# A new order of the steps of a windowed attention, with merged visits of P times V and four PSUM tiles that are allocated once

## The chip, the cores and the metric

The kernel runs on one core of one Trainium2 chip. The metric is device time in microseconds (us) for one execution. Three runs of the kernel before took 691.85, 692.1 and 692.67 us; their median, 692.1 us, is the time before.

## What is computed

From an input x of 2048 tokens by 512 features the program computes two branches and mixes them by a gate:

```
qkv = x @ wqkv                       # 32 heads of 16 features
scores = q k^T / 4, each token sees itself and the 255 tokens before it
a = softmax(scores) @ v  ->  @ wo
b = gelu(layernorm(x) @ w1 + b1) @ w2 + b2      # 512 -> 1792 -> 512
g = sigmoid(sum(x * gate_w));  out = g * a + (1 - g) * b
```

All of it is in 32-bit floats.

## The kernel before

The program has three stages. The first makes q, k and v and writes q and k to DRAM in stacks. The second is attention, and it is where the change lies. The third multiplies the hidden layer by w2, the attention's result by wo, and writes the output. The third begins when the second's last matmul is through.

The attention stage handles four heads at a time, in eight chunks (`p` from 0 to 7), and 2048 tokens in 16 blocks of 128. It consists of four kinds of step, which TensorE executes in the order of the letters of the string `ORDER` (`run`, L735). The order is thus written out by hand, and it is static: TensorE goes through it in sequence, and a step that waits holds all behind it.

- **S** (`s_pair`, L348) multiplies q of one block with the keys that it sees, 128 to 384 columns, for two heads side by side. VectorE then finds the largest score of each row: a masked copy (L366) and a maximum (L367), or, for the first two blocks of a chunk, two calls of L363 with a read-out each. After each four blocks `put_max` (L371) sends the maxima through POOL, VectorE and DRAM back into the stacks, 6, 13, 21 and 28 steps later (`CHAIN`).
- **T** (`st_pair`, L403) multiplies k with q, transposed, with the maxima already in the product. ScalarE takes the exponential (L414) and POOL masks it (L416).
- **P** (`pv`, L423) multiplies the exponentials with v, for two blocks of queries (a group `j` of eight), 256 columns. Each product is a real 32-bit one, which the trace records as two passes, and four heads go side by side in columns of the array, 32 wide. ScalarE copies the 256 columns to SBUF (VectorE in the last chunk).
- **f** (`fill`, L706) is one of 24 steps of a unit of the hidden layer (`mlp1_unit`, L626; 28 units): two matmuls of 512 columns, which use the two halves of the array's rows. The units hang on nothing in attention, so their steps fill the time in which the others wait.

In all there are 256 T, 236 S (20 more stand in the first stage), 64 P and 672 f. One P is run behind the string, and the last 14 f after it.

The results lie in PSUM in four pairs of banks, `b0` to `b3`. A running unit of f holds one pair; S, T and P take the others in turn, from a list `ring`, whose next entry a digit of the string `PICK` chooses. Each use allocates a new tile on its pair (`ps`, L103), which waits until those who used the pair's former tile are through.

Of the kernel before, what the change touches and what calls it, by code (L numbers as in the profile page):

```python
# [13 lines left out]
F32R = mybir.dt.float32r  # L14
# [23 lines left out]
ORDER = ("TfSfSfffffTfSfffTSfffTfSfffTSfffTfSffSPTSffTfSfffTSfffSPSTfSfffTfSfTffTffTSffTfffTSPSSTPSTfTfffTSffT"
         "ffSffTSffffTSfffTfSffTfSfffSPSTSPTffSTffTfffTfSTffffTSffTfSfffTSfffTfSffSPSSTPTffTSffTffSffTfSfffTSf"
         "ffTfSfffTSfffTfSfSPSTTPTTSPSSTPSffTSffffSTfffTffSffTfSfffTfSffTfSfffSPSTTffffSTffTfffSTffTfffSSPfSfT"  # L40
         "ffSffTfTfffTSPSSTPTffTSfffTfSffTfSffffTSfffTfSffTffSffTPfSSPTffSfTfSffTfSfTffTffSTfffSffTfSfffTSfffS"
         "PTSTPSTSPTffTSffTffSffTSffffTSffffSTfffTffTfSfSfPSSTPfSfTfSfffTfTffSfTfSffffTSfffTfSffffTfSPSTSPTfSf"
         "ffTSfffTfSffTfSfffTfSfTfffTSfTffffTSPTTSPSTSPfTfSTfffSfffTSfffTfSffTfSfffTSfffTfSffSPPSTffTfffSTffTf"
         "ffTfSTfffSfTffTfSffTfSfffSPSSTPSffTfSfffTSfffTfSfffTSfffTfSfffTSffffSPPfSTfTfffSfTffTfSffTffTfSffTff"
         "SfTfTffffSPTTSPSTSPSfffTSfffTfSffTfSffffTSfffTfSffTfSfffSPfSTfTffffTfSTfffTfSfffTSfffTfSffTfSfffSPTS"
         "SPPTSTffffTfSTfffSffTfSfffTSfffTfSffTfffSfSPTSTPSSfTffffTfSffTfSfffTSfffTfSfffTSfffffSTPTTSPTSffTffS"
         "ffTfSfffTSfffTffSfTfTfffSTfTfffSPSSSPPSTSffffTfSfffTSfffTfTfffSTfffTffSTffffSPSTSPSTffTfffSTffTffTSf"
         "ffSffTSfffTfSffTfSfffSPSTSPfTfSTfffTffTSfffTfSfffTSfffTfSffTfSfffSPTTSPSTSPTffTSffTfSfffTfSfffSSfffT"
         "ffffTSffTfSffSPSffTSfffTfSffTfSffSTfffTffTffTfTffffTfPPTTTPfTffTffTffTPPTfTfffTffTfffTTffTfffTfPfTTf"
         "TTffffP")  # L50
PICK = ("0000000000000000001000000000000000000001000100100000000000000000100001000100000000000001000000000000"
        "0000000000000100010000010000000000001001001000101010001000100000000000000000001000000000100000000000"
        "0010000000000001000010020101010000000000100101000000000000000010000001000010000000000000000100100010"
        "1000000000100000000000000000000000000000000000000001000000000000000000010001000000000000001000000100"
        "0000000000000000100000000000000000000000000001001100000010010000000010010000000010000010000000000010"
        "00010000000000000000000101000100000100000000000000010000000000000000000000000000000")
# [5 lines left out]
def gated_mix_kernel(ctx, tc: tile.TileContext, xt, x2, wq0, wqk, wv, wo, xa, gw, w1, w2, b1, b2, out):  # L62
    nc = tc.nc
    dve, act, pool, pe, sp = nc.vector, nc.scalar, nc.gpsimd, nc.tensor, nc.sync
# [38 lines left out]
    def ps(tag, shape=(128, 512)):  # L103
        key, bufs = banks[tag]
        return left[key].tile(list(shape), F32, name=nm("ps_" + tag), tag=tag, bufs=bufs)

    ring, picks = [], list(PICK)

    def choose():
        return ring.pop(int(picks.pop(0)) if picks else 0)  # L110

    def two():
        if not ring:
            return ps("x", (128, 2, 512))
        ring.append(choose())
        return ps(ring[-1], (128, 2, 512))

    def small(tag, bufs, shape, dt=F32):
        return consts.tile(list(shape), dt, name=nm(tag), tag=tag, bufs=bufs)

    def view(t, *ap, off=0):
        return bass.AP(tensor=t.tensor, offset=t.offset + off, ap=[list(x) for x in ap])

    def f32(t):
        return t.bitcast(F32)

# [17 lines left out]
    spot = [None]  # L144
    soons = {}
# [224 lines left out]

    def put_max(p, a):  # L371
        mx = mxs[p][:, :, :, a:a + 4]
        m = small("nm", 2, (128, 2, 2, 2, 4), F32R)
        ms = small("ms", 2, (128, 32))
        md = dram.tile([2, 2, 2, 4, 128], F32R, name=nm("md"))

        def parts():
            pool.tensor_copy(m[:, 0], mx)
            lo_part(m[:, 1], mx, m[:, 0], pool)

        def turn():
            dve.transpose(ms, f32(m).rearrange("p a b c d -> p (a b c d)"))

        def put(eng=None):
            (eng or (act if spot[0] > 99 else sp)).dma_start(f32(view(md, [32, 4], [128, 32], [1, 32])), ms)

        def rest():
            done.add(("m", p, a // 4))
            for k in range(2):
                src = view(md, [512, 2], [1024, 2], [1, 512], off=2048 * k)  # L390
                sp.dma_start(f32(qk[62 + k:113 + k:50, :2, a * 128:a * 128 + 512]), f32(src))

        if spot[0] is None:
# [26 lines left out]
        while late:  # L420
            late.pop(0)()

    def pv(p, j, last):  # L423
        flush()
        a = two()[:, 0]
        parts = ((-1, 0, 128, 256), (-2, 0, 256, 128), (0, 0, 0, 256), (1, 128, 0, 128))[0 if j else 2:]
        for n, (d, at, fr, w) in enumerate(parts):
            kb = 2 * j + d
            for h in range(4):
                v = (4 * p + h) * VW  # L430
                pe.matmul(a[32 * h:32 * h + 32, at:at + w], vs[:, kb, v:v + 32], pts[p, kb][:, h, fr:fr + w],  # L431
                          start=n == 0, stop=n == len(parts) - 1, skip_group_check=True, tile_position=(0, 32 * h))
        if j % 2 == 0:
            sums.append(sums.pop(0))
            acc[p] = sums[-1]
        s = acc[p]
        o = j % 2 * 256
        if last:
            dve.tensor_copy(s[:, o:o + 256], a[:, :256])
        else:  # L440
            copy(s[:, o:o + 256], a[:, :256])
        if j % 2:
            to = osc[p, :, (j - 1) * 256:(j + 1) * 256]
            if lt:
# [180 lines left out]

    def mlp1_unit(f, cp):  # L626
        held = choose()
        o = ps(held, (128, 2, 512))
        w = w1t[f]
        n = 0  # L630
        for k, i in ((0, 0), (1, 0), (0, 1)):
            for kt in range(KT):
                y = ys[cp, i, kt // 4]
                a = kt % 4 * C
                m = kt % 4 * 128
                for e in range(2):
# [95 lines left out]
    ls = [(p, qb, pr) for p in range(8) for qb in range(NB) for pr in range(2)][2 * (NB - LAG):]  # L732
    lp = [(p, j) for p in range(8) for j in range(NB // 2)]

    def run(order):  # L735
        for a in order:
            spot[0] += 1
            for fn in soons.pop(spot[0], []):
                fn()
            flush()  # L740
            if a == "T":
                p, kb, pr = lt.pop(0)
                if not pr:
# [137 lines left out]
    for n in range(len(seq)):  # L881
        tick()
        for k in (n + 6,):
            c, f = item(k)
# [4 lines left out]
        c, f = item(n + 1)  # L889
# [6 lines left out]
        c, f = seq[n]  # L896
# [52 lines left out]
```

## Time and profile before

| | before |
|---|---|
| median of three runs | 692.1 us |
| span of the profiled execution | 687.8 us |
| first stage, to the first step of attention | 144.3 us |
| attention | 343.5 us |
| third stage | 200.0 us |
| TensorE busy | 680.8 us, 99% |
| VectorE, ScalarE, POOL busy | 69%, 56%, 39% |
| granted clock of TensorE | 9 tenths or more in each of 40 slices |

The profile comes from one execution, with a span of 687.8 us; the median of the runs shown stands 4.3 us above it, and those 4.3 us lie outside of what the profile covers. Since matmuls overlap and their ends are modelled, TensorE's busy time hides short waits. They are seen better in the starts of its instructions: a step that begins later than the step before it needs has waited.

### The profile page before, as it was taken

Reading aid. Unit: us, or ns where it says so; the run is one execution under the profiler, and the core shown is the slowest. Engines: PE = TensorE matmul, PEld = TensorE weight load, DVE = VectorE, ACT = ScalarE, POOL = GpSimd, SP = SyncE. Lnnn points to the kernel's source line nnn. Section 1 sums busy time; section 2 is a strip of 40 time slices with the busy share of each in tenths; the row PEclk is TensorE's granted clock in tenths of the full one; section 3 lists DMA queues with packets and bytes.
Section 4 is the critical chain, followed back from the end, with each engine's and each line's share of the span. In section 5 each row is a group of like instructions: output and inputs, shape, how many; then the busy total and the mean of one; then the engine's idle time right before and its main releaser. Section 6 shows DMA issues by size and latency. Waiting matters only on the chain.

```text
span 687.8 us, 15782 instructions
## 1 busy us (share of the span) xinstructions
PE 680.8 (99%) x5738; PEld 536.9 (78%) x5738; DVE 474.4 (69%) x972; ACT 384.9 (56%) x639; POOL 267.1 (39%) x622
## 2 busy tenths in 40 slices
PE   9999999999999999999999999999999999999997
PEld 6887777877877777778787877777788888888886
DVE  6737779967877878778587777866575545556454
ACT  6437453457677686876867767678633224123131
POOL 5800156426566665755666655658000000000000
PEclk9999999999999999999999999999999999999999
DMA  8999887796665758656776555526786450831801
GB/s 313 363 311 267 252 268 248 225 276 203 208 195 171 228 179 261 195 155 229 219 229 190 173 184 167 190 96 218 272 261 199 140 172 5 270 132 44 250 1 62
DMA packets 89621, 137.92 MB, mean 201 GB/s; under 512 B 13160, under 2 KB 36648, under 8 KB 89416
## 3 DMA queue, kind: packets, MB, share of 16 engines
q1 hardware_dynamic: 81384, 128.72, 58.5%
q10 hardware_dynamic: 8160, 8.19, 4.0%
q8 instruction: 46, 0.75, 0.5%
q14 instruction: 31, 0.25, 0.1%
HBM read 81.53 MB, written 54.30 MB: 197 GB/s over the span
## 4 chain that ended last, share of the span: by engine, by line
PE 95%; ACT 2%; DMA 1%; DVE 1%; POOL 1%; issue 0%; SPq 0%; DVEq 0%; ACTq 0%
PE ps_a L858 22%; PE ps_b L638 22%; PE ps_d L303 12%; PE ps_b L431 12%; PE ps_d L333 7%; PE ps_b L412 6%; PE ps_o L827 6%; PE ps_b L357 6%; PE ps_d L290 1%; PE ps_x L357 1%; DMA wv<-in_wq 1%; ACT pb L414 0%; DMA md<-ms 0%; DVE us L872 0%; ACT x L414 0%; ACT t L131 0%
## 5 line engine op out<-in xcount | busy, mean ns | idle before, releaser
L638 PE MATMUL ps_b<-x,w 64*128 64x512 f32 x1344 | 210.8, 395 | 0.2 <-ACT pb L414 0.2
L858 PE MATMUL ps_a<-x,t 128*128 128x512 f32 x648 | 149.7, 389 | 0.0
L367 DVE TENSOR_REDUCE mx<-ps_b 128x2 f32<-128x512 f32 x208 | 144.0, 692 | 7.2
L858 PEld LDWEIGHTS ps_a<-x,t 128*128 128x128 f32 x648 | 121.6, 188 | 25.3
L638 PEld LDWEIGHTS ps_b<-x,w 64*128 64x128 f32 x1344 | 129.0, 186 | 11.2 <-issue 2.0
L366 DVE COPY_PREDICATED ps_b<-tri,ps_b 128x256 f32<-128x256 uint8 x208 | 88.2, 424 | 43.7 <-PE ps_b L357 32.6
L416 POOL TENSOR_SCALAR_AFFINE_SELECT pa<-pa 128x256 f32<-128x256 f32 x192 | 74.3, 415 | 66.7 <-ACT pa L414 66.2
L414 ACT ACTIVATE pa<-ps_b 128x768 f32<-128x768 f32 x96 | 76.6, 813 | 25.6 <-PE ps_b L412 18.9
L412 PE MATMUL ps_b<-qk 64*128 64x384 f32 (+5 forms) x512 | 88.6, 338 | 0.8 <-DMA qk<-md 0.3
L303 PE MATMUL ps_d<-x,w 128*128 128x512 f32 x360 | 84.7, 390 | 0.0
L357 PE MATMUL ps_b<-qk 62*128 62x384 f32 (+2 forms) x472 | 82.5, 343 | 0.2
L303 PEld LDWEIGHTS ps_d<-x,w 128*128 128x128 f32 x360 | 67.3, 188 | 14.5 <-issue 0.5
L416 POOL TENSOR_SCALAR_AFFINE_SELECT pb<-pb 128x256 f32<-128x256 f32 x160 | 62.7, 420 | 39.1 <-ACT pb L414 37.1
L414 ACT ACTIVATE pb<-ps_b 128x768 f32<-128x768 f32 (+2 forms) x96 | 65.5, 706 | 17.2 <-PE ps_b L412 12.0
L694 ACT ACTIVATE t<-t,b1s 128x512 f32<-128x512 f32 x56 | 38.5, 716 | 45.3 <-DMA t<-hp 44.8
L412 PEld LDWEIGHTS ps_b<-qk 50*128 50x128 f32 (+1 forms) x512 | 50.4, 184 | 17.3 <-issue 4.2
L416 POOL TENSOR_SCALAR_AFFINE_SELECT x<-x 128x256 f32<-128x256 f32 x128 | 49.9, 420 | 26.4 <-ACT x L414 26.0
L414 ACT ACTIVATE x<-ps_b 128x768 f32<-128x768 f32 x64 | 51.1, 813 | 13.4 <-PE ps_b L412 10.1
L357 PEld LDWEIGHTS ps_b<-qk 62*128 62x128 f32 (+1 forms) x472 | 45.2, 184 | 16.1 <-issue 3.6
L333 PE MATMUL ps_d<-wv,x 128*128 128x512 f32 x192 | 46.7, 394 | 0.0
L827 PE MATMUL ps_o<-w,t 128*128 128x512 f32 x192 | 46.1, 389 | 0.0
L431 PE MATMUL ps_b<-pa,v 128*32 128x256 f32 (+1 forms) x768 | 43.3, 330 | 0.2 <-POOL x L416 0.2
(96 smaller groups left out, 755.9 us busy)
## 6 DMA issues: line engine op xcount, KB each, us to landing
qk<-qk SPq DMA_DIRECT2D x112, 196.0 KB
t<-hp SPq DMA_DIRECT2D x56, 256.0 KB
hp<-t SPq DMA_DIRECT2D x54, 256.0 KB
qk<-t SPq DMA_DIRECT2D x48, 256.0 KB
osc<-x SPq DMA_DIRECT2D x31, 256.0 KB
t<-in_w SPq DMA_DIRECT2D x28, 256.0 KB
w<-w SPq DMA_DIRECT2D x28, 256.0 KB
qk<-t ACTq DMA_DIRECT2D x24, 256.0 KB
```

The costliest lines, as they stand in the source:

```text
L303: pe.matmul(o, a[:, dt * 128:(dt + 1) * 128], b[:, dt * C:(dt + 1) * C], start=n == 0, stop=n == 11)
L333: pe.matmul(o, x[:, a:a + 128], wvs[dt][:, k], start=n == 0, stop=n == 11)
L357: pe.matmul(o[:, e, :n], qs[pr][r:k, qb * 128:qb * 128 + 128], ks[pr][r:k, t0:t0 + n], start=True, stop=True)
L366: dve.copy_predicated(o[:, :, :128], tri, o[:, :, 256:384])
L367: dve.tensor_reduce(m, o[:, :, :256], mybir.AxisListType.X, ALU.max)
L412: pe.matmul(o[:, e, :w], ks[pr][r:k, kb * 128:kb * 128 + 128], qs[pr][r:k, kb * 128:kb * 128 + w], start=True, stop=True)
L414: act.activation(pt[:, :, :w], o[:, :, :w], AF.Exp, scale=0.25)
L416: pool.affine_select(out=pt[:, :, a:a + 128], in_=pt[:, :, a:a + 128], pattern=[[0, 2], [sgn, 128]], base=b, channel_multiplier=-sgn, comp ...
L431: pe.matmul(a[32 * h:32 * h + 32, at:at + w], vs[:, kb, v:v + 32], pts[p, kb][:, h, fr:fr + w], start=n == 0, stop=n == len(parts) - 1, sk ...
L638: pe.matmul(o[:, e], w[kt // 4][r:r + 64, k, m:m + 128], y[r:r + 64, a:a + C], start=n == 0, stop=n == 23)
L827: pe.matmul(a, x[:, g], wos[g][:, k], start=n == 0, stop=n == 11)
L858: pe.matmul(accs[c][b], x[:, b * 128:(b + 1) * 128], w, start=f == 0 and n == 0, stop=f == FT - 1 and n == 2)
```

## The change

The two strings are new ones. `ORDER` has the same letters in the same numbers (652 f, 256 T, 236 S, 63 P) in another sequence, and `PICK` chooses other banks.

When two P follow each other and the first has an even `j`, they are run as one: `pv` gets `both`, computes 512 columns in one bank with six products in place of eight (four in place of six where `j` is 0), and ScalarE copies the 512 columns in one instruction. In the new string this holds at three places, each of them the groups 0 and 1 of a chunk (chunks 4, 6 and 7).

The four pairs of banks are allocated once, at their first use (`pair`), and then written again as the same tile. `put_max` allocates its two small tiles when they are written and not when the step is reached, and `run` calls all functions that are due at a place or before it, since a merged visit counts for two.

```diff
-ORDER = ("TfSfSfffffTfSfffTSfffTfSfffTSfffTfSffSPTSffTfSfffTSfffSPSTfSfffTfSfTffTffTSffTfffTSPSSTPSTfTfffTSffT"
+ORDER = ("TSTffffSffTSffffTSfffTfSffTffSffTfSfffSPffTSffTffSffSPTfSTfffTffSTffSfTffSTffSffTSfPSTSPTffSTfffSffT"
...
-    ring, picks = [], list(PICK)
+    ring, picks, pairs = [], list(PICK), {}
+
+    def pair(tag):
+        if tag not in pairs:
+            pairs[tag] = ps(tag, (128, 2, 512))
+        return pairs[tag]
...
         ring.append(choose())
-        return ps(ring[-1], (128, 2, 512))
+        return pair(ring[-1])
...
-        m = small("nm", 2, (128, 2, 2, 2, 4), F32R)
-        ms = small("ms", 2, (128, 32))
+        sm = {}
...
-    def pv(p, j, last):
+    def pv(p, j, last, both):
         flush()
         a = two()[:, 0]
-        parts = ((-1, 0, 128, 256), (-2, 0, 256, 128), (0, 0, 0, 256), (1, 128, 0, 128))[0 if j else 2:]
+        if both:
+            parts = ((-1, 0, 128, 256), (-2, 0, 256, 128), (0, 0, 0, 384), (1, 128, 0, 384), (2, 256, 0, 256),
+                     (3, 384, 0, 128))[0 if j else 2:]
+        else:
+            parts = ((-1, 0, 128, 256), (-2, 0, 256, 128), (0, 0, 0, 256), (1, 128, 0, 128))[0 if j else 2:]
...
-        if last:
+        if both:
+            copy(s, a)
+        elif last:
             dve.tensor_copy(s[:, o:o + 256], a[:, :256])
...
     def mlp1_unit(f, cp):
         held = choose()
-        o = ps(held, (128, 2, 512))
+        o = pair(held)
...
+                p, j = lp.pop(0)
+                skip = b == "P" and j % 2 == 0
+                if skip:
+                    lp.pop(0)
+                pv(p, j, not ls, skip)
+                spot[0] += skip
```

Three places of TensorE's order show what moves. In the rows, L638 and L651 are f, L357 and L362 are S, L412 and L418 are T, L431 and L441 are P (lines before and after the change); the digit behind `ps_b` is the pair of banks, and x4 counts equal instructions. Two equal rows of f stand for one step.

The first place is the start of chunk 4's P, before the change two visits on two pairs of banks (b2 and b0):

```order
L638 MATMUL ps_b1_706_4613<-x8_171_1021,w_572_3687 128x512 x8
L357 MATMUL ps_b3_721_4747<-qk_3_79 128x384 x2
L431 MATMUL ps_b2_725_4755<-pa_255_1523,v_4_80 32x256 x4
L431 MATMUL ps_b2_725_4755<-pa_255_1523,v_4_80 32x128 x4
L431 MATMUL ps_b0_726_4765<-pa_255_1523,v_4_80 32x256 x4
L431 MATMUL ps_b0_726_4765<-pa_255_1523,v_4_80 32x128 x4
L431 MATMUL ps_b0_726_4765<-x8_253_1521,v_4_80 32x256 x4
L431 MATMUL ps_b0_726_4765<-pa_255_1523,v_4_80 32x128 x4
L638 MATMUL ps_b1_727_4783<-x8_193_1143,w_571_3686 128x512 x2
```

With the change the same two groups of chunk 4 are one visit, on b0 alone:

```order
L651 MATMUL ps_b2_262_1541<-x8_171_1021,w_358_3470 128x512 x8
L362 MATMUL ps_b3_263_1547<-qk_3_79 128x384 x2
L362 MATMUL ps_b1_261_1536<-qk_3_79 128x384 x2
L441 MATMUL ps_b0_260_1530<-pa_255_1523,v_4_80 32x384 x8
L441 MATMUL ps_b0_260_1530<-x8_253_1521,v_4_80 32x256 x4
L441 MATMUL ps_b0_260_1530<-pa_255_1523,v_4_80 32x128 x4
L362 MATMUL ps_b2_262_1541<-qk_3_79 128x128 x2
L418 MATMUL ps_b3_263_1547<-qk_3_79 128x384 x2
L651 MATMUL ps_b1_261_1536<-x8_193_1143,w_357_3469 128x512 x6
L362 MATMUL ps_b0_260_1530<-qk_3_79 128x128 x2
```

Six groups of four products became four, of the same 1152 columns, and b0 is used again six steps later.

The second place is the end of the string, the last T of chunk 7, on TensorE before the change:

```order
L412 MATMUL ps_b2_1091_7352<-qk_3_79 128x256 x2
L412 MATMUL ps_b3_1092_7357<-qk_3_79 128x256 x2
L638 MATMUL ps_b1_1061_7140<-x8_212_1256,w_874_5787 128x512 x2
L412 MATMUL ps_b0_1095_7374<-qk_3_79 128x128 x2
L412 MATMUL ps_b2_1096_7379<-qk_3_79 128x128 x2
L638 MATMUL ps_b3_1097_7384<-x8_193_1143,w_931_6234 128x512 x8
L431 MATMUL ps_b1_1098_7393<-pa_255_1523,v_4_80 32x256 x4
```

The same four T with the change:

```order
L418 MATMUL ps_b1_261_1536<-qk_3_79 128x256 x2
L418 MATMUL ps_b0_260_1530<-qk_3_79 128x256 x2
L651 MATMUL ps_b3_263_1547<-x8_193_1143,w_465_5770 128x512 x4
L418 MATMUL ps_b2_262_1541<-qk_3_79 128x128 x2
L651 MATMUL ps_b3_263_1547<-x8_193_1143,w_465_5770 128x512 x4
L418 MATMUL ps_b1_261_1536<-qk_3_79 128x128 x2
L651 MATMUL ps_b3_263_1547<-x8_193_1143,w_465_5770 128x512 x8
```

Before, b2 and b3 are taken again one and two steps behind the T that used them; with the change five steps lie between the two uses of b1, and f runs on b3, which neither T has.

The third place is the first S of chunk 2 with the P next to it, shown with the semaphores that each instruction waits for, on TensorE before the change:

```order
L357 MATMUL ps_b3_400_2514<-qk_3_79 128x128 [waits DMAHW7_49,DMAHW6_49,Activation_49]
L357 MATMUL ps_b3_400_2514<-qk_3_79 128x128
L638 MATMUL ps_b0_382_2381<-x8_212_1256,w_233_1370 128x512 x2
L357 MATMUL ps_b1_408_2531<-qk_3_79 128x128 [waits DVE_49,PE_49]
L357 MATMUL ps_b1_408_2531<-qk_3_79 128x128
L431 MATMUL ps_b2_411_2538<-pa_255_1523,v_4_80 32x256 [waits Activation_49,Pool_49]
```

And with the change:

```order
L362 MATMUL ps_b1_261_1536<-qk_3_79 128x128 [waits DMAHW7_49,DMAHW6_49,Activation_49]
L362 MATMUL ps_b1_261_1536<-qk_3_79 128x128
L651 MATMUL ps_b3_263_1547<-x8_212_1256,w_233_1370 128x512 x4
L362 MATMUL ps_b2_262_1541<-qk_3_79 128x128 [waits DVE_49]
L362 MATMUL ps_b2_262_1541<-qk_3_79 128x128
L362 MATMUL ps_b0_260_1530<-qk_3_79 128x256 [waits Activation_49]
L362 MATMUL ps_b0_260_1530<-qk_3_79 128x256
L441 MATMUL ps_b1_261_1536<-pa_255_1523,v_4_80 32x256 [waits DVE_49,Pool_49]
```

P took b2 from a T before, and takes b1 from an S now, four steps behind that S. The wait for TensorE's own semaphore is gone from the second S: over the whole program 263 of TensorE's instructions wait for two semaphores or more before the change, and 125 with it.

## Rows read from the trace of the kernel before

**Rows 1.** The page: busy us of the engines, and TensorE's granted clock in 40 slices.
```profile
PE 680.8 (99%) x5738; PEld 536.9 (78%) x5738; DVE 474.4 (69%) x972; ACT 384.9 (56%) x639; POOL 267.1 (39%) x622
...
PEclk9999999999999999999999999999999999999999
```
**Rows 2.** The page's chain of waits, by line, shares of the span.
```profile
PE ps_a L858 22%; PE ps_b L638 22%; PE ps_d L303 12%; PE ps_b L431 12%; PE ps_d L333 7%; PE ps_b L412 6%; PE ps_o L827 6%; PE ps_b L357 6%; PE ps_d L290 1%; PE ps_x L357 1%; DMA wv<-in_wq 1%; ACT pb L414 0%; DMA md<-ms 0%; DVE us L872 0%; ACT x L414 0%; ACT t L131 0%
```
**Rows 3.** The three stages: length, busy us by engine, clock, DMA share, GB/s.
```profile
0.00:144.30 144.30, 142.62 (x626) 111.30 (x626) 104.07 (x197) 72.31 (x157) 56.66 (x70) 1.00 0.88 280
144.30:487.80 343.50, 342.01 (x4250) 263.59 (x4249) 260.89 (x588) 249.88 (x384) 210.44 (x552) 1.00 0.62 196
487.80:687.80 200.00, 196.13 (x866) 162.02 (x864) 109.46 (x187) 62.70 (x98) 0.00 (x0) 1.00 0.47 151
```
**Rows 4.** TensorE's timeline around one P: start us, length, instructions.
```profile
423.44 0.86 PE L638 MATMUL ps_b<-x,w 64*128 64x512 f32 x6
424.12 0.36 PE L357 MATMUL ps_b<-qk 62*128 62x384 f32 x2
424.41 0.64 PE L431 MATMUL ps_b<-pa,v 128*32 128x256 f32 x8
424.86 0.40 PE L431 MATMUL ps_b<-x,v 128*32 128x128 f32 x8
425.08 0.61 PE L431 MATMUL ps_b<-pb,v 128*32 128x256 f32 x8
425.51 0.40 PE L431 MATMUL ps_b<-x,v 128*32 128x128 f32 x8
425.84 0.45 PE L357 MATMUL ps_b<-qk 62*128 62x384 f32 x2
426.13 0.34 PE L412 MATMUL ps_b<-qk 64*128 64x384 f32 x2
426.31 0.34 PE L357 MATMUL ps_b<-qk 62*128 62x384 f32 x2
```
**Rows 5.** TensorE's timeline at two P in a row, first and next step.
```profile
401.34 0.64 PE L431 MATMUL ps_b<-pa,v 128*32 128x256 f32 x8
...
404.08 0.44 PE L357 MATMUL ps_b<-qk 62*128 62x384 f32 x2
```
**Rows 6.** TensorE's timeline at the last T.
```profile
477.68 0.24 PE L412 MATMUL ps_b<-qk 64*128 64x128 f32 x2
478.25 0.33 PE L412 MATMUL ps_b<-qk 64*128 64x128 f32 x2 [0.33 <-ACT pb L414]
478.74 1.20 PE L638 MATMUL ps_b<-x,w 64*128 64x512 f32 x8 [0.16 <-ACT pb L414]
```
**Rows 7.** TensorE's timeline at a T of chunk 1.
```profile
213.25 0.66 PE L638 MATMUL ps_b<-x,w 64*128 64x512 f32 x4
214.26 0.45 PE L412 MATMUL ps_b<-qk 64*128 64x384 f32 x2 [0.35 <-DMA qk<-md]
```
**Rows 8.** TensorE's timeline at the first S of chunk 2.
```profile
201.64 0.33 PE L357 MATMUL ps_b<-qk 62*128 62x128 f32 x2
202.18 0.86 PE L431 MATMUL ps_b<-pa,v 128*32 128x256 f32 x16 [0.21 <-POOL x L416]
```
**Rows 9.** ScalarE's copies out of PSUM: busy us, mean ns, idle before.
```profile
L131 ACT ACTIVATE t<-ps_b 128x512 f32<-128x512 f32 x54 | 29.4, 599 | 3.3 <-PE ps_b L638 3.2
L131 ACT ACTIVATE x<-ps_b 128x256 f32<-128x256 f32 x56 | 21.6, 385 | 30.0 <-PE ps_b L431 28.3 <-ACT t L131 1.1 <-ACT pb L414 0.5
```
**Rows 10.** VectorE's work for narrow S, in attention.
```profile
L363 DVE CUSTOM_DVE_ANT_0 scr<-ps_b,wide 128x256 bf16<-128x256 f32 x28 | 10.8, 422 | 10.2 <-PE ps_b L357 10.2
L363 DVE CUSTOM_DVE_ANT_0 scr<-ps_b,wide 128x128 bf16<-128x128 f32 x28 | 7.0, 288 | 4.4 <-PE ps_b L357 4.2
...
L363 DVE DVE_READ_ACCUMULATOR2_ANT mx<- 128x1 f32 x56 | 4.6, 83 | 0.0
```
**Rows 11.** Semaphore waits that stand alone on TensorE's queue before S: ns min/median/max.
```profile
L357 PEldq EVENT_SEMAPHORE  x130: 51/51/849, 48.2 to 456.2; - x130
```

More of the change, by code (lines that the diff above doesn't have):

```diff
@@ L37 @@
 U8 = mybir.dt.uint8
-ORDER = ("TfSfSfffffTfSfffTSfffTfSfffTSfffTfSffSPTSffTfSfffTSfffSPSTfSfffTfSfTffTffTSffTfffTSPSSTPSTfTfffTSffT"
[L39 to L56, printed above, removed]
+ORDER = ("TSTffffSffTSffffTSfffTfSffTffSffTfSfffSPffTSffTffSffSPTfSTfffTffSTffSfTffSTffSffTSfPSTSPTffSTfffSffT"
+         "fSfffTSfffTfSfffTSfffTfSffSPTTSPTSfTfffSfTfTfffSTfTffSfTffSfffTSfffTfSffSPSTSPTSTfffTffSTffSfffTSfff"
+         "fTSfffTfSffTffSffSSPTTSPTTSPSSTPSffTfSfffTfSffTfSffffTSfffTfSffTffTffSPSTSPSffTfSfffSTfffTffTfSfTffS"
+         "ffTffSfTfTfffSTPSTTPPSTfffTffSTffSfffTSffffTSfffTfSffTfSfffSPSTffSfTffSTfffSfTSfffTfSffTfSfffTSffffT"
+         "fSPTSTPSSTPSffTfSfffSTfffTffSffTfSfffTSfffTfSfffSPTSTPSTffTfTffSTfffSffTfSfffTSfffTfSffTfffSfSPPTSff"
+         "TffTffSTfffTffSTfffSffTSffTffSTfffSfSPTSTPSSTPSfffTSffffTSffTffSffTffSffSfTfffTfffTSPSSTPTffSffTfSff"
+         "fSfTffTffTffSTfTffSffTSffffSPTSTPTffSTffTfffTSffTffSffffSTfffSffTffffSSPPSTfffSTffSfTffTfSffTfffSTff"
+         "fTffSTfffTffSPSTTPTSTPTSffTffSffTfSffffTSfffTffSfTffSffTffSfSPSffSfTfffTfSfffSfTfffSffTSffffTfSffSfP"
+         "STSPPTSffTffSffTfSfffTSffffSTffSfffTSffSffTSfPTSTPTSfffTfSffTfSfffTSffffTSffTffSffTSffffSPTSTPSTffTf"
+         "ffSTffTfffTSfffTffSfTffSfffTTfffSSPPTSTPTSffTffSffTfSfffTSffffTSfffTfSffTfffSfSPPSTfffTffSTfffSffTSf"
+         "fTfSfTffSfTfSffTfSfffSPSTSPSffTSffffTfSfffTfSffTfSfffTfSffTffffSTPSSTPTffSTfffTffSTffSffTffTfSffTfSf"
+         "ffSTfffSfPSTTPTSfffTfSffTffSffTSffffTSffffSTffTffffTTPPTfffTfffTTPTTffTfPPTTffTffffTfffTfTffTfffTPPT"
+         "TffTffT")
@@ new lines @@
+PICK = ("0000000000000000000100000000100000000000001010010000000000000000000000100110000000000010100000100000"
+        "0000010000100010001100000000000000100101000010001010100000010000100100000000000000000000000000000100"
+        "0000011000010000000000000100110010000000000010000001001001000000000000011000000000010001000110000010"
+        "0010000000000000100000010000000000000000100100100100000000000000001010001001000100000010010100000000"
+        "0010010000000000000000000000000000000100100000101000010000000000000000000000010010010000000000001010"
+        "00000000000000000110010010100000101001000000000000010000000000000000000000001000")
@@ L372, in put_max @@
         mx = mxs[p][:, :, :, a:a + 4]
-        m = small("nm", 2, (128, 2, 2, 2, 4), F32R)
-        ms = small("ms", 2, (128, 32))
+        sm = {}
         md = dram.tile([2, 2, 2, 4, 128], F32R, name=nm("md"))
         def parts():
+            m = sm["m"] = small("nm", 2, (128, 2, 2, 2, 4), F32R)
             pool.tensor_copy(m[:, 0], mx)
@@ L381, in turn @@
         def turn():
-            dve.transpose(ms, f32(m).rearrange("p a b c d -> p (a b c d)"))
+            sm["s"] = small("ms", 2, (128, 32))
+            dve.transpose(sm["s"], f32(sm["m"]).rearrange("p a b c d -> p (a b c d)"))
         def put(eng=None):
-            (eng or (act if spot[0] > 99 else sp)).dma_start(f32(view(md, [32, 4], [128, 32], [1, 32])), ms)
+            (eng or (act if spot[0] > 99 else sp)).dma_start(f32(view(md, [32, 4], [128, 32], [1, 32])), sm["s"])
         def rest():
@@ L441, in pv @@
             copy(s[:, o:o + 256], a[:, :256])
-        if j % 2:
+        if j % 2 or both:
+            j += both
             to = osc[p, :, (j - 1) * 256:(j + 1) * 256]
@@ L735, in run @@
     def run(order):
-        for a in order:
+        skip = False
+        for a, b in zip(order, order[1:] + " "):
+            if skip:
+                skip = False
+                continue
             spot[0] += 1
-            for fn in soons.pop(spot[0], []):
-                fn()
+            for n in sorted(n for n in soons if n <= spot[0]):
+                for fn in soons.pop(n):
+                    fn()
             flush()
@@ L748, in run @@
             elif a == "P":
-                pv(*lp.pop(0), not ls)
+                p, j = lp.pop(0)
+                skip = b == "P" and j % 2 == 0
+                if skip:
+                    lp.pop(0)
+                pv(p, j, not ls, skip)
+                spot[0] += skip
             else:
```

## The prediction

> **What bounds the kernel now.** I read the page first. TensorE is busy for 680.8 of 687.8 us, no other engine for more than 69%, and its granted clock is at the upper of its two levels, 2.4 GHz, throughout [rows 1]. The chain of waits that ended last is TensorE's nearly from end to end, by the lines of its matmuls [rows 2]. The table by stage puts 343.5 us into attention, between 144.3 us of the first stage and 200.0 us of the third, whose code the change leaves alone [rows 3]. So the time is the sum of TensorE's steps in attention and of the waits between them, and I read the steps off its timeline by their starts.
>
> Three f take 424.12 − 423.44 = 0.68 us, so one takes 0.227. A T of 384 columns takes 426.31 − 426.13 = 0.18. In a P, four products side by side take 425.51 − 425.08 = 0.43 us at 256 columns and 425.08 − 424.86 = 0.22 at 128 [rows 4], so a P costs by columns: 2 × (0.43 + 0.22) = 1.3 us for the full form, 0.65 for group 0.
>
> Around a P something is added. The S ahead of it takes 424.41 − 424.12 = 0.29 us and not 0.18; so does the S behind it, 426.13 − 425.84. And the P itself takes 425.84 − 424.41 = 1.43 [rows 4], while two in a row take 404.08 − 401.34 = 2.74, that is 0.12 less than twice 1.43 [rows 5]. An unbroken run of P therefore costs 0.11 + 0.12 + 0.11 = 0.34 us, once, however many P it holds.
>
> The floor of the stage, from the steps' numbers: 672 f × 0.227 = 152.5; 432 S and T of 384 columns × 0.18 = 77.8; 60 narrower ones, at 0.227 us per 512 columns, 5.1; 56 full P × 1.3 and 8 × 0.65, 78.0; 58 runs of P × 0.34 = 19.7. That is 333.1 of 343.5 us. About 10 us are waits and small delays, and that is all that an order can win beyond the runs of P.
>
> **The change, part by part.** *Runs of P.* Counted in the strings, with the P behind them, the P stand in 58 unbroken runs before and in 55 now. Three runs less save 3 × 0.34 = 1.0 us, all on TensorE's path.
>
> *Merged visits.* They save 24 products, 48 recorded passes. In the rows the time of a P is proportional to its columns, 0.43 against 0.22 us for twice the columns [rows 4], and 1152 columns are streamed in either form. I take 0; the bounds are 0 and 3 × 0.3 us saved, if the two narrow groups that go at each place had cost 0.15 us beyond their columns. The Trainium skill (TensorEngine Tiling (Array Packing), Instruction Overhead) gives each matmul about 60 cycles of overhead, so that one of few columns takes as long as one of 60; at 2.4 GHz and 48 passes an estimate from that page is 1.2 us, and the sum would be 688.6. The proportional rows speak against it.
>
> The copy of a merged visit takes 599 ns in place of two of 385 [rows 9]: ScalarE gains 0.17 us three times, off the path. The bank comes free 0.21 us later. At chunk 4 the next user of b0 comes six steps on, behind S, T and three f, over 0.9 us, which covers 0.6. I take 0; without that cover it costs 3 × 0.21 = 0.6 us. The same page (PSUM Bottleneck) warns that column tiling speeds up TensorE but not the emptying of PSUM, which speaks against one wide copy; by it the sum would be 690.3, and the order shows the cover.
>
> *Waits that go.* At the last T of chunk 7, TensorE needs 0.57 and 0.49 us for two steps of 128 columns, a quarter of an f or 0.06 each, because their banks were still with the exponential [rows 6]: 0.94 us. In the new order the pair is used again after five steps, and f has another pair. This wait goes, and nothing stands close behind it: six f, 1.4 us, separate the last T from the last P, which needs its exponential and its mask first.
>
> At 214.26 a T waits for the maxima: 1.01 us for two f, 0.55 too much [rows 7]. By the two strings the T stood 42 steps behind the S that releases the maxima, and stands 45 behind it now; from the step that sends them to DRAM (21 behind the S) to the T I count 5.85 us of steps before and 6.43 now. The 0.58 gained covers 0.55. No other T has less than 6.0 now, and before one with 6.07 came without a wait.
>
> *Waits that stay or come.* At the first S of chunk 2 P waited: 0.54 us for an S of 0.06 plus 0.11, so 0.37 [rows 8]. Now P takes the bank of an S that VectorE needs 2 × 288 + 2 × 83 = 742 ns for [rows 10], 0.64 us behind it. I leave 0.37. Elsewhere old tight places go and new ones come. Counting places where a pair is taken again with less than 0.25 us to spare beyond its reader's duration, I find 19 before and 24 now. I take 0, with ±2 us as bounds.
>
> *Tiles allocated once.* 263 instructions of TensorE waited for two or more semaphores, 125 do now. An extra wait stands alone on the queue for 51 ns [rows 11]. But the S at 424.12 has one (its semaphores are VectorE's and TensorE's), and the f ahead of it still took 0.227; the S at 426.31 has two, and the T ahead took 0.18 [rows 4]. They lie beside running matmuls. I take 0, and keep 154 × 0.051 = 7.9 us as the far bound (154 such waits fewer in the built program). ScalarE gets 88 more; it is busy for 250 of 343.5 us [rows 3], so I take 0 there too.
>
> *The sum,* against the profiled execution: 687.8 − 1.0 − 0.94 − 0.55 = 685.3 us, and with the 4.3 us by which the median stands above that span, 689.6 us, 0.4% less.
>
> **The rivals.** *Queue relief.* If the lone waits do delay weight loads behind them, part of the 7.9 us and of the 10 us of small delays goes as well: half of the 7.9 gives 685.7. For it speaks that some f begin late without a named wait; against it the steps of rows 4, at full pace behind one or two such waits. 14%.
>
> *Nothing left.* The new tight places cost what the old ones did and 2 us more: 691.6, no change that can be told. For it: 24 against 19; ScalarE's queue carries more waits, and a late exponential holds a bank. 25%.
>
> *Banks from narrow S (slower).* Adding up the steps above between the end of an S and the next use of its pair, I find 13 places in the new order with less than 1.16 us, down to 0.64; in the old one 1.16 is the least. The narrow S allow for it, which need 742 ns of VectorE, or 2 × 422 + 2 × 83 = 1010 [rows 10]. But whatever stands in VectorE's queue ahead comes on top. If each place then holds TensorE for 0.6 us, 7.8 us come and the time is 697.4. It decides from 0.3 us a place: 13 × 0.3 = 3.9 us is the gain of 2.5 and the 1.4 that cannot be told. For it: VectorE is busy for 261 of 343.5 us [rows 3]. Against it: beyond the 742 or 1010 ns, ten of the 13 places leave 0.12 us or more, and from one S to the next TensorE has 343.5 / 236 = 1.45 us of steps on average. 14%.
>
> **How the numbers follow.** A measurement of this kernel can tell 0.2%, 1.4 us, from no change. My forecast has 47%: 689.6, its own range 688.2 to 691.2. Faster by over 0.2% are most of it (43 of 47) and the queue relief (14): 57%. Within 0.2% are the rest of it and the second rival, but for 3 of its 25 that end slower: 26%. Slower are the third rival and those 3: 17%. The range takes in half of the first rival, all of the second, and the third up to 2 us over the time before: 686.2 to 694.0.
>
> **What would show it.** In the new trace the S ahead of and behind a P should still take 0.29 us, and two P in a row 2.74; a merged visit of groups 0 and 1 should take 2.0 to 2.1. The last T should show no wait for ScalarE, and no T a wait of over 0.1 us for the maxima. Attention should last 341 us and the third stage 200.0. If attention lasts over 344 us, look at S with narrow tiles and the step that takes their bank; if under 338, at TensorE's lone waits. I am wrong if a T waits for ScalarE at places that have room in the order, or if the third stage changes by more than 0.5 us.

## The result, and the profile after

The changed kernel takes 694.93 us (median of 20 runs, 691.91 to 700.54), the kernel before in the same series 692.32 us (20 runs, 689.85 to 694.92). The ratio is 1.0038, 95% interval 1.0023 to 1.0054: slower by 2.6 us, where 689.6 and faster was forecast. The profiled execution took 692.18 us, its span is 690.5 against 687.8 before. In all 111 executions of the two kernels whose span is on record the time lies 1.7 to 1.8 us above the span; so the profiled execution before took some 689.5 us, about as little as the shortest of its 20 runs, and the one after is near its shortest too.

The three stages again (length, busy us of TensorE, its weight loads, VectorE, ScalarE and GpSimd, granted clock, DMA share, GB/s):

```profile
0.00:144.26 144.26, 143.00 (x626) 111.76 (x626) 105.09 (x197) 72.59 (x157) 56.88 (x70) 1.00 0.88 281
144.26:489.90 345.64, 341.44 (x4201) 262.43 (x4201) 259.92 (x586) 251.34 (x383) 211.00 (x552) 1.00 0.62 194
489.90:690.50 200.60, 196.67 (x866) 161.98 (x864) 109.72 (x188) 62.71 (x98) 0.00 (x0) 1.00 0.48 151
```

Against [rows 3] attention is longer by 2.1 us, the third stage by 0.6. I split attention once more from start to start of TensorE's steps, at the prices of the prediction. What exceeds a step's price is a wait, given to the step behind it. T(4,10) is the T of chunk 4, block 10; the others are named alike.

| us of attention | before | after |
|---|---|---|
| steps at their price | 333.42 | 332.47 |
| T waits for maxima from DRAM | 0.55 | 1.52: T(1,10) 0.32, T(2,10) 0.18, T(4,10) 1.02 |
| S waits for columns from DRAM | 0 | 1.59: S(3,10) 0.21, S(4,2) 0.88, S(6,6) 0.49 |
| the end: last T before, P(7,6) after | 0.94 | 3.02 |
| all other waits | 8.19 | 6.69 |
| sum | 343.1 | 345.3 |

The first row is a count at fixed prices, with three runs of P less. That the price still holds is seen in the new trace: around a run of P, 0.34 us come on top of the columns in the median of the 55 runs (0.35 in the 58 before). So what the order was to bring came: 0.95 us of steps, and in these two executions 1.5 us of small waits on top. Two kinds of wait took 4.6 us back.

The largest is at the end. TensorE's timeline there (start us, length, line, instructions, and in brackets the idle time before and who ended it):

```profile
478.23 1.06 PE L441 MATMUL ps_b<-pb,v 128*32 128x256 f32 x8
479.38 0.41 PE L441 MATMUL ps_b<-x,v 128*32 128x128 f32 x4
481.67 0.41 PE L441 MATMUL ps_b<-x,v 128*32 128x128 f32 x4 [1.87 <-POOL x L422]
482.01 0.50 PE L418 MATMUL ps_b<-qk 64*128 64x256 f32 x4
```

This is P(7,6), and its last four products wait for the mask of T(7,13). The chain of waits in this stretch (start us, us, what) says why the mask is late:

```profile
477.06 0.61 ACT t L136
477.67 0.02 issue
477.69 2.07 DMA hp<-t
...
479.84 0.04 ACT t L136
479.88 0.45 issue
480.33 0.81 ACT x L420
481.15 0.06 issue
481.20 0.42 POOL x L422
481.62 0.04 issue
481.67 0.41 PE ps_b L441 x4
```

The two `ACT t L136` are ScalarE's copies of the two halves of f unit 26. The second begins only when the first half's write to DRAM (`hp<-t`, 2.07 us) has landed, and the exponential of T(7,13) (`ACT x L420`) stands behind it in ScalarE's queue. In the program both halves have the same work tile. Five of the six work tiles are held at that point by loads whose consumers come later in program order. Before the change unit 26 ended behind the T of block 14, its halves got two tiles, and the two copies ran in one piece:

```profile
478.57 1.09 ACT L131 ACTIVATE t<-ps_b 128x512 f32<-128x512 f32 x2
```

The second kind is waits for DMAs. At T(4,10), ScalarE's queue sends the maxima, SP's queue loads them back, and TensorE waits:

```profile
334.10 0.53 ACTq L391 DMA_DIRECT2D md<-ms  x1
```
```profile
338.88 1.35 SPq L397 DMA_DIRECT2D qk<-md  x2
```
```profile
341.85 0.62 PE L418 MATMUL ps_b<-qk 64*128 64x384 f32 x4 [0.86 <-DMA qk<-md]
```

From the end of the sending to the loading back pass 4.25 us here. For these same maxima it was 2.80 us before the change; over all 32 transfers it is 1.4 to 5.7 us before (median 2.7) and 1.4 to 5.6 after (median 3.2). At T(1,10), whose one wait [rows 7] I had taken for all places, it was 2.66 us before and 3.32 after.

The packets show what these 4.25 us are made of. The first of the transfer's 128 packets starts 1.93 us after the sending, the last ends 1.68 us later, at 338.24, and 0.65 us after that the loading back begins. Meanwhile the 16 DMA engines are busy 0.92 of the time (the last but one figure), nearly all of it with other transfers:

```profile
334.63:338.24 3.61, 3.61 (x38) 3.33 (x36) 2.20 (x8) 3.10 (x5) 3.05 (x10) 1.00 0.92 285
```

Of the 56 transfers that ScalarE's queue sends in the two profiles, the last packet ends 1.0 to 4.0 us after the sending: 1.15 us in the median of the 10 with the engines under 0.5 busy, 3.19 in that of the 16 with over 0.85. The longest time to a loading back after the change, 5.6 us, is of another sort: its packets are through after 1.5 us, and the loading back stands in SP's queue behind a load of columns that waits for TensorE.

And at S(4,2), it is the columns of the next chunk: SP's queue, then TensorE.

```profile
283.32 0.82 SPq L664 DMA_DIRECT2D hp<-t  x2
284.23 0.40 SPq L458 DMA_DIRECT2D osc<-x  x1
284.72 2.09 SPq L349 DMA_DIRECT2D qk<-qk  x4
```
```profile
289.39 0.41 PE L651 MATMUL ps_b<-x,w 64*128 64x512 f32 x2
290.50 0.44 PE L362 MATMUL ps_b<-qk 62*128 62x384 f32 x2 [0.70 <-DVE mx L368]
```

The columns' last reader, T(3,3), ended at 282.6. The load was issued 2.1 us later, behind two writes of f's halves and one of a P, and landed at 290.37, 7.8 us after that reader's end. Up to S(4,2) there are 7.94 us, 0.88 of them the wait. Before the change the same load was issued 2.3 us after its reader's end and landed 6.9 us after it, with 8.56 us up to S(4,2): the queue held it as long then, but the steps gave it 1.5 us more and it landed sooner. The program's wait there is for the two DMAs of these columns and for VectorE, which was through with the bank at 289.38; the row names VectorE all the same.

### The profile page after: what moved, and what is told of

It is laid out like the page before. It is cut to its first block, busy times and chain, and to the rows that moved or that the text cites. A ratio compares the mean times of both kernels' runs of the same rounds, so it can differ in the third digit from the quotient of the medians.

```text
span 690.5 us, 15620 instructions
## 1 busy us (share of the span) xinstructions
PE 681.1 (99%) x5690; PEld 536.2 (78%) x5690; DVE 474.7 (69%) x970; ACT 386.6 (56%) x638; POOL 267.9 (39%) x622
## 2 busy tenths in 40 slices
DMA packets 89620, 137.91 MB, mean 200 GB/s; under 512 B 13160, under 2 KB 36648, under 8 KB 89416
## 3 DMA queue, kind: packets, MB, share of 16 engines
q10 hardware_dynamic: 8160, 8.19, 4.0%
## 4 chain that ended last, share of the span: by engine, by line
PE 93%; DMA 3%; DVE 1%; ACT 1%; SPq 0%; issue 0%; DVEq 0%; POOL 0%; ACTq 0%
PE ps_a L881 22%; PE ps_b L651 20%; PE ps_d L308 12%; PE ps_b L441 12%; PE ps_d L338 7%; PE ps_b L418 6%; PE ps_o L850 6%; PE ps_b L362 6%; DMA md<-ms 2%; PE ps_d L295 1%; PE ps_x L362 1%; PE ps_x L279 1%; DMA qk<-md 1%; DMA qk<-qk 0%; ACT pb L420 0%; DVE x L133 0%
## 5 line engine op out<-in xcount | busy, mean ns | idle before, releaser
L651 PE MATMUL ps_b<-x,w 64*128 64x512 f32 x1344 | 206.7, 393 | 0.0
L651 PEld LDWEIGHTS ps_b<-x,w 64*128 64x128 f32 x1344 | 126.9, 186 | 9.4 <-DVE mx L372 0.2
L420 ACT ACTIVATE pa<-ps_b 128x768 f32<-128x768 f32 x96 | 76.9, 812 | 25.5 <-PE ps_b L418 15.0
L418 PE MATMUL ps_b<-qk 64*128 64x384 f32 (+5 forms) x512 | 88.7, 341 | 1.2 <-DMA qk<-md 1.0
L362 PE MATMUL ps_b<-qk 62*128 62x384 f32 (+3 forms) x472 | 82.2, 341 | 1.1 <-DVE mx L368 0.7
L420 ACT ACTIVATE pb<-ps_b 128x768 f32<-128x768 f32 (+2 forms) x96 | 66.2, 706 | 18.9 <-PE ps_b L418 11.7
L418 PEld LDWEIGHTS ps_b<-qk 64*128 64x128 f32 (+1 forms) x512 | 49.2, 184 | 17.6 <-issue 3.5
L420 ACT ACTIVATE x<-ps_b 128x768 f32<-128x768 f32 x64 | 51.6, 813 | 15.9 <-PE ps_b L418 9.5
L362 PEld LDWEIGHTS ps_b<-qk 62*128 62x128 f32 (+1 forms) x472 | 45.2, 184 | 16.7 <-issue 3.2
L441 PE MATMUL ps_b<-pa,v 128*32 128x128 f32 (+2 forms) x720 | 43.2, 341 | 0.0
```

The costliest lines, as they stand in the source:

```text
L362: pe.matmul(o[:, e, :n], qs[pr][r:k, qb * 128:qb * 128 + 128], ks[pr][r:k, t0:t0 + n], start=True, stop=True)
L418: pe.matmul(o[:, e, :w], ks[pr][r:k, kb * 128:kb * 128 + 128], qs[pr][r:k, kb * 128:kb * 128 + w], start=True, stop=True)
L420: act.activation(pt[:, :, :w], o[:, :, :w], AF.Exp, scale=0.25)
```

## The experiments

Theory 1: the end of attention, by ScalarE's queue. Theory 2: waits of S and T for DMAs. Theory 3: the tiles allocated once cost time by their waits. Each kernel was timed beside the kernel before.

| kernel | median us | before beside it | ratio, 95% interval |
|---|---|---|---|
| e1 weights one block later | 692.60 | 691.70 | 1.0009 (0.9987 to 1.0031) |
| e2 maxima sent earlier | 696.57 | 691.70 | 1.0067 (1.0045 to 1.0089) |
| e3 new order, tile per use | 696.23 | 691.70 | 1.0067 (1.0040 to 1.0094) |
| e4 old order, tiles once | 693.87 | 691.70 | 1.0026 (1.0006 to 1.0046) |
| e5 new order, no column loads | 688.81 | 691.99 | 0.9959 (0.9941 to 0.9977) |
| e6 old order, no column loads | 690.80 | 691.99 | 0.9979 (0.9962 to 0.9997) |
| e7 last P but one later | 691.00 | 691.99 | 0.9984 (0.9963 to 1.0005) |
| e8 columns in halves | 694.85 | 691.99 | 1.0058 (1.0035 to 1.0081) |
| e9 less ahead of the maxima | 690.11 | 692.27 | 0.9976 (0.9952 to 0.9999) |
| e10 as e9, tile per use | 692.37 | 692.27 | 1.0012 (0.9991 to 1.0032) |

**e1, a work tile for each half.**

```diff
-        if p == 7 and kb == 13:
+        if p == 7 and kb == 14:
             early_wo(0, 2)
```

> The changed kernel, but the two weight tiles of the output projection are loaded one block of chunk 7 later, so that the two halves of unit 26 of f get two work tiles and not the same one twice. Theory 1 (the loss sits at the end of attention: ScalarE's copy of the second half waits for the first half's write to DRAM, 2.18 us, and holds the exponential that P(7,6) needs behind it): that copy no longer waits for a DMA, the exponential starts near 478.3 instead of 480.33, its mask ends near 480.1 because GpSimd is busy until 479.7, and the 3.0 us wait inside P(7,6) falls to about 1.3; the time falls by 1.7 us, to about 693.2. Theory 2 (the loss is waits of S and T for DMAs): the same DMA waits stay, 2.3 us or more in sum, and the time moves by under 0.7 us. Theory 3 (the tiles allocated once cost time by their waits): no change.

The end of attention, all engines but the weight loads:

```profile
476.42 1.12 ACT L136 ACTIVATE t<-ps_b 128x512 f32<-128x512 f32 x2
477.38 0.87 ACT L420 ACTIVATE x<-ps_b 128x768 f32<-128x768 f32 x1
478.72 1.49 POOL L422 TENSOR_SCALAR_AFFINE_SELECT x<-x 128x256 f32<-128x256 f32 x4
479.91 0.41 PE L441 MATMUL ps_b<-x,v 128*32 128x128 f32 x4 [0.31 <-POOL x L422]
480.25 0.50 PE L418 MATMUL ps_b<-qk 64*128 64x256 f32 x4
```

The two copies now run in one piece, the exponential starts at 477.38 in place of 480.33, and the wait falls from 3.02 to 1.45 us. The ratio goes from 1.0038 to 1.0009, 2.0 us where 1.7 were expected; the two intervals overlap by a little, but 1.6 us of it are seen at this very place. Theory 1 holds for this part of the loss. GpSimd is what the rest waits for: its masks run without a pause up to 480.2.

**e2, maxima sent earlier.**

```diff
-CHAIN = (6, 13, 21, 28)
+CHAIN = (6, 12, 17, 24)
```

> The changed kernel, with the steps at which the maxima are transposed, sent to DRAM and loaded back set to 12, 17 and 24 behind the S that releases them, in place of 13, 21 and 28. Theory 2, as far as it concerns the maxima: the waits of the first T of chunks 1, 2 and 4 that need them (0.32, 0.18 and 1.02 us) go, 1.5 us, and the time falls to about 693.4; S(3,10), S(4,2) and S(6,6) still wait for their columns. Theory 1: the 3.0 us inside P(7,6) stay and the time stays at 694.9 within 0.7. Theory 3: no change.

A miss: 2 us slower than the changed kernel by the ratios. T(4,10) and T(1,10) wait no more, but T(2,10) waits 0.54 us, T(5,2) 1.19, and chunk 0 has new waits, the largest at P(0,0). There (ScalarE, then TensorE) a copy of weights waits 1.90 us for its load, and the exponential stands behind it:

```profile
153.69 0.63 ACT L136 ACTIVATE w<-t 128x512 fp32r<-128x512 f32 x1 [1.90 <-DMA t<-in_w]
154.23 0.79 ACT L420 ACTIVATE pa<-ps_b 128x768 f32<-128x768 f32 x1
155.16 0.70 PE L441 MATMUL ps_b<-pa,v 128*32 128x256 f32 x9 [1.50 <-ACT pa L420]
```

Shifting the small transfers for all chunks moves waits; it does not remove them. (The profiled execution took 699.59 us, 3 us over this kernel's median, so its waits are on the long side.) This run also shows what follows a long wait. The end of attention in slices of 0.5 us (length, TensorE's busy us and instructions, granted clock, DMA share, GB/s):

```profile
486.00:486.50 0.50, 0.00 (x0) 1.00 0.05 20
486.50:487.00 0.50, 0.14 (x4) 1.00 1.01 393
487.00:487.50 0.50, 0.50 (x8) 1.00 1.05 402
487.50:488.00 0.50, 0.50 (x9) 1.00 0.62 234
488.00:488.50 0.50, 0.50 (x6) 0.53 0.00 0
488.50:489.00 0.50, 0.50 (x4) 0.50 0.00 0
...
491.00:491.50 0.50, 0.50 (x6) 0.55 0.84 324
491.50:492.00 0.50, 0.50 (x10) 1.00 0.03 8
```

TensorE stood still in P(7,6) up to 486.86, and at about 488.0, with work running again, its clock fell to the lower level, 1.2 GHz, until 491.5. Seven f there took 1.6 us over their price.

**e3 and e4, the tiles.** e3 puts `ps(...)` back in place of `pair(...)` in `two()` and `mlp1_unit`; e4 puts `pair(...)` into the kernel before.

> The changed kernel's order, picks and shared visits, but a PSUM tile allocated at every use, as before. Theory 3 (tiles allocated once cost time): the time falls to 692.3 or less, and TensorE's waits of over 0.15 us become fewer. Theories 1 and 2 (the order is what costs): within 0.7 us of 694.9, with the wait of 2 to 3 us inside P(7,6) and the waits of S and T for DMAs still there.

> The kernel before, with its order and picks and a visit for each P, but four PSUM tiles allocated once. Theory 3: 694 us or more. Theories 1 and 2: 692.3 within 0.7, with the waits of before (0.55 us at a T of chunk 1, 0.94 at the last T). The prediction took 0 for this edit, with a gain of up to 7.9 us as its far bound: 684.4 would show that bound.

e3 does not bring the time back; by the ratios it is 2.0 us slower still. Theory 3 as the cause of the loss falls, though the 0.7 us that theories 1 and 2 allowed are exceeded too. By an estimate as in the next section, 1.4 of the 2.0 us go with the clock: its mean is 0.9956 over these runs and 0.9976 over those of the changed kernel. In its profile, of an execution 4.4 us over its median, the wait inside P(7,6) is 4.21 us, and S(3,10) waits 3.14 for its columns:

```profile
271.89 0.44 PE L362 MATMUL ps_b<-qk 62*128 62x384 f32 x2 [2.98 <-DMA qk<-qk]
```

The granted clock is 0.50 from 273.0 to 276.0 and again behind P(7,6). e4 is 1.8 us slower than before, more than the 0.7 allowed; on the base of the expectation that is 694.1, which theory 3 had asked for. The profile shows 0.9 us more in attention (344.0), in new waits of 0.2 to 0.5 us for ScalarE, while the 0.55 us at T(1,10) did not come; its first stage is 3.7 us longer with the same code. So the 0 that I took for this edit does not hold for the old order, and a gain of 7.9 us is excluded in both. Why the tiles cost there and do not with the new order stays open.

**e5 and e6, both orders without the DMAs.** In both, `load_stacks` and the loading back of the maxima are issued for chunk 0 alone; e5 has e1's edit too.

> The changed kernel with the weight tiles of the output projection one block later (as in the first experiment), and without the loads of columns and maxima for chunks 1 to 7: S and T of all chunks work on the columns of chunk 0, so its values are not the reference's. No S and no T then waits for a DMA. Theory 2 (beside the end of attention, it is waits for DMAs that turned the gain into a loss): against the old order with the same loads left out (sent beside it) it is 2.0 us faster: 1.0 by three runs of P less, 1.5 by fewer small waits, and 0.5 lost where P(7,6) still waits 1.44 us and the last T of before 0.94. Theory 3 (the tiles allocated once, or the order itself, cost time without any DMA): the same as the old order, or slower.

> The kernel before, without the loads of columns and maxima for chunks 1 to 7; its values are not the reference's either. All theories: only 0.55 us of named DMA waits go (the T of chunk 1), so about 1 us faster than the kernel before, 690.7 to 691.7. It is the base that the new order without these loads is held against.

Attention in e5, then in e6 (columns as in the stages above):

```profile
144.89:485.06 340.17, 339.63 (x4201) 262.99 (x4200) 258.82 (x582) 250.88 (x383) 209.52 (x552) 1.00 0.41 130
```
```profile
148.40:491.05 342.65, 341.44 (x4249) 265.05 (x4249) 260.60 (x588) 249.63 (x384) 209.51 (x552) 1.00 0.40 129
```

688.81 against 690.80 us, 2.0 us as expected; in the stage itself 2.5, of which 0.95 are steps and 2.0 small waits, and 0.5 are lost at the end. (That e6's stage begins 3.5 us later comes from the first stage, whose code all these kernels share; 2.1 us of it are two waits of S for VectorE near 102 us.) Without these transfers the new order is the faster one, by about what the prediction had summed up beside the maxima, though not by its terms. With them, and with e1's edit, it is not (1.0009). e1 and e5 have the same order, and where their steps part is seen one by one: attention is 3.5 us longer in e1, 2.7 of them at four places that wait for a DMA there, S(4,2) 0.92, T(5,2) 0.85, T(4,10) 0.59 and S(3,10) 0.37. So the DMA waits take the gain, and the end of attention makes it a loss. Theory 2 holds beside theory 1. Both runs also show what made the small transfers slow: with the DMA engines 0.41 and 0.40 busy in attention in place of 0.62, the last packet of the maxima ends 1.0 us after the sending in the median, in place of 2.2 before and 2.3 after the change.

**e7, the rest of the end.** e1's edit, and the string's end in another order, with the picks that keep the banks apart:

```diff
-"...TPPTTffTffT"
+"...TPTTffffPTT"
```

> The first experiment's kernel, with the end of the string in another order: P(7,6) stands behind the T of block 14 and four f, and no more directly behind P(7,5). Theory 1 (what was left of the loss at the end is that P(7,6) comes before GpSimd has masked the tile of T(7,13)): its wait of 1.44 us falls under 0.2, the run of P that is broken costs 0.34, and the time falls by about 1.0 us against the first experiment, to 691.6 on the same base of 691.7 to 692.3. If the wait only moves to the last T or to P(7,7), the time stays at 692.6.

P(7,6) on TensorE, from its first product to the T behind it:

```profile
479.89 0.64 PE L441 MATMUL ps_b<-pa,v 128*32 128x256 f32 x8
480.35 0.40 PE L441 MATMUL ps_b<-x,v 128*32 128x128 f32 x8
480.56 0.61 PE L441 MATMUL ps_b<-pb,v 128*32 128x256 f32 x8
481.00 0.52 PE L441 MATMUL ps_b<-x,v 128*32 128x128 f32 x8
481.45 0.44 PE L418 MATMUL ps_b<-qk 64*128 64x128 f32 x4
```

1.56 us and no named wait; 0.35 us went to the first of the four f ahead, which takes a bank that VectorE still copies out. 691.0 us, 1.6 under e1 by the medians where 1.0 was expected; the intervals of the two overlap. T(4,10) waited 1.64 us in this run.

**e8, the columns in halves.** One `load_stacks` of 128 columns at each block in place of 256 at every second.

> The seventh experiment's kernel, with the columns of the next chunk loaded 128 at a time, one block earlier for the first half, in place of 256 at every second block: twice the DMAs, the same bytes. Theory 2: the first S of a load gets a block, some 2.3 us, more distance, the waits at S(3,10), S(4,2) and S(6,6) (0.37 to 0.92 us) go, and the time is 1.5 us under the seventh's. Rival: the queue that issues them is held up for longer by twice the DMAs, and rows of 512 bytes take the DMA engines longer, so that the maxima and the columns come later: slower than the seventh by 1 us or more.

The rival was right: 3.9 us over e7, of which by the same estimate 1.4 go with the clock (a mean of 0.9972 over the runs, 0.9992 with e7). No S waits for columns any more, but T waits longer for DMAs: T(4,10) 2.63 us, T(0,10) 1.41 and T(1,2) 1.00. Here T(4,10):

```profile
345.25 0.61 PE L418 MATMUL ps_b<-qk 64*128 64x384 f32 x4 [2.47 <-DMA qk<-md]
```

**e9 and e10, less ahead of the maxima.** In e9 the two copies from DRAM to DRAM of blocks 6 and 8 of chunk 4 come in blocks 10 and 12; e10 is e9 with a tile per use.

> The seventh experiment's kernel; the two copies of 256 KB from DRAM to DRAM that blocks 6 and 8 of chunk 4 issue come in blocks 10 and 12. They stood right ahead of the maxima of chunk 4: sent at 334.4 us, these could be loaded back only at 338.7, and T(4,10) waited 1.0 to 2.6 us in the runs so far. Theory 2 (small transfers queue behind bulk transfers that the order puts ahead of them): 0.5 MB less at some 300 GB/s is 1.7 us, so the maxima are loaded back near 337, T(4,10) waits under 0.3 us, and the time falls by 1 us against the seventh, to 0.997 of the kernel before. If landing takes its 4 us whatever stands ahead, the wait stays over 1 us and the time is the seventh's.

> The ninth kernel, with a PSUM tile allocated at every use as before. Experiment 4 was 0.26% slower than before by tiles allocated once, experiment 3 0.29% slower by taking them away again. If tiles allocated once cost by themselves, this one is 1.8 us faster than the ninth; if they win by themselves, 2.0 us slower; if both results came from how the DMAs fell (theory 2), it stays within 0.7 us of it.

690.11 us, 0.9976: the one version of the reference's computation whose interval stays under 1, if barely; from e7, with 0.9963 to 1.0005, it can't be told. The reason given for it failed. The maxima were loaded back 4.47 us after they were sent, and T(4,10) waited 1.27 us:

```profile
336.15 1.38 SPq L349 DMA_DIRECT2D qk<-qk  x2
340.31 1.38 SPq L397 DMA_DIRECT2D qk<-md  x2
```

So those two copies alone don't make the landing slow here: without them the first packet still starts 1.86 us after the sending, the last ends 1.86 us later, and the DMA engines are 0.93 busy meanwhile. The other traffic fills them. e10 is 0.36% slower than e9, as e3 was than the changed kernel by 0.29%, while e4 went the other way. By the expectation that is what tiles allocated once would win with the new order. But e10's profiled execution, the shortest of its 12, had 340.4 us of attention and waited 0.41 at T(4,10), where e9's had 343.3; whether the tiles win or the DMAs fell otherwise, the runs don't settle.

## Why the prediction was wrong

- **Runs of P, 1.0 us: right.** Three runs less, and each of the others still costs 0.34 us in the new trace.
- **Merged visits, 0: right as far as the trace shows;** no run leaves them out. The three took 2.08 us each, as forecast, and none of the next ten steps waits over 0.1 us, so the wide copy cost nothing either. (That a wide copy is the worse one is the prediction's own inference, not a statement of the Trainium skill. The sums beside the two estimates are slips: 689.6 less 1.2 is 688.4, and with 0.6 more it is 690.2.) Here the visit of chunk 4, and the S behind it:

```profile
328.62 1.50 PE L441 MATMUL ps_b<-pa,v 128*32 128x384 f32 x16
329.94 0.61 PE L441 MATMUL ps_b<-x,v 128*32 128x256 f32 x8
330.37 0.40 PE L441 MATMUL ps_b<-pa,v 128*32 128x128 f32 x8
330.70 0.33 PE L362 MATMUL ps_b<-qk 62*128 62x128 f32 x2
```

- **The last T's wait, 0.94 us: gone, but "nothing stands close behind it" was the first step that failed.** (By the listed order six steps lie between the two uses of b1, and before three lay between those of b2 and of b3.) I looked from the last T to the last P and not at the P before it. P(7,6) came with only P(7,5) between it and the last T of block 13, whose exponential and mask it needs; in ScalarE's queue stood a copy with a shared work tile. That place costs 3.02 us, 2.1 more than the wait that went; e1 and e7 took it away in two pieces.
- **The maxima: "The 0.58 gained covers 0.55. No other T has less than 6.0 now" was the second.** T(1,10) still waited 0.32 us, and T(4,10), with the same 6.43 us of steps, 1.02. One place's need was taken for all, while the time from the sending to the last packet alone spreads over 3 us. "Before one with 6.07 came without a wait" was one draw.
- **The columns were left out, the third step that failed.** I counted steps from the sending of maxima to T, but not from T(p,kb) to the first S on the next chunk's columns. Counted the same way, from the start of T(p,kb), the old order has at least 7.5 us there, the new one 5.7, and 16 of 56 places have under 7.0. With the maxima these waits grew by 2.6 us, as much as the whole of the forecast gain.
- **Small waits, 0 with ±2 us: they fell by 1.5,** and by 2.0 between e6 and e5. 24 tight places in place of 19 said nothing about them; that they helped was luck.
- **The rivals.** Banks from narrow S: in the profile after, no S with narrow tiles waited over 0.12 us, and of the steps that take its bank only S(4,2) did, for its columns as shown above; in e5, without the loads, it does not wait. So the advice to look there if attention lasts over 344 us pointed to the wrong place. Queue relief: not seen. The loss had no rival that named it: both slower cases were of banks, none of DMAs or of a queue in order.
- **Third stage.** "More than 0.5 us" was too tight as a sign: it lasts 200.0 to 202.2 us in these profiles, with the same code but for e1's one block.
- **The base of the sum.** Of the 4.3 us between median and span only 1.7 lie outside of the profile; the other 2.6 are that the profiled execution was a short one. So the waits read from it may be fewer than those of a usual run.

The clock adds to it. Of the changed kernel's 20 runs, 9 have a mean granted clock under 0.998 (mean 0.9976); of the 91 runs of the kernel before beside the experiments, 3 (0.9995). At half speed the work lost is that share of the span, an estimate of 0.0019 × 693 = 1.3 us in the mean. With e1 it is 1 run of 12 (0.9992), with e3 10 of 12 (0.9956). The profiled execution of the changed kernel, with a wait of 1.87 us in one piece there, shows no fall, so the 2.1 us more of attention in it are the waits alone; 0.6 are in the third stage and stay unexplained. The Trainium skill (TensorE: Matmul & The Clock Gate, HAM oscillation — how this bites in real kernels) says that a wait for a DMA between stretches of matmuls can let the clock drop, so that the work behind it starts slow. The rows of e2 and e3 agree in part: the clock did fall behind long waits, but 0.4 to 1.2 us after the work had begun again at the upper level, and only one of the three waits was for a DMA, the other two for a mask. The prediction had no term for it.

## What to carry to other kernels

When an order is rewritten, count the distance for every producer that stands behind it in some queue in order: banks, but also ring buffers (in program order, who still holds them), the copies ahead of an exponential, and each DMA that an instruction needs. For a transfer, take the longest landing that the trace shows, not the one at the place that you look at. An order with less slack can win by the sum of its steps and lose by its tail of waits, the more so where a long wait lowers TensorE's clock: compare the spread of the runs, not only one trace.

## What the runs showed of the hardware

- A transfer of 16 KB to DRAM took 1.0 to 4.0 us from the end of its sending to the end of its last packet, in one and the same kernel, by and large the longer the busier the DMA engines were: 1.15 us in the median with the engines under 0.5 busy, 3.19 with over 0.85, and 1.0 in e5 and e6, which leave out the loads of columns. The loading back came 0.4 us or more after that. The Trainium skill (DMA: Bandwidth & Descriptors, Anatomy of one DMA — SWDGE (gpsimd) path) gives about 2 us as the fixed part of a DMA on GpSimd's path. These went by ScalarE's queue, and the least of them was loaded back 1.43 us after its sending.
- TensorE's clock fell to its lower level shortly after work had begun again behind a wait, not during it: in e2 at 488.0 us, with work from 486.86 on, in e3 at 272.7, with work from 271.89 on.
- Halving the columns of a load (e8 against e7) raised the packets from 89,620 to 113,141 at the same 137.9 MB, and the time by 3.9 us.
